# Turning the MLP's input block by block on the chip, and storing it turned, in an FNet layer with a channel MLP

## The chip, the cores and the metric

One core of a Trainium2 chip runs the whole layer as one program. The metric is the device time of one execution in microseconds (us). Profiled executions add a trace: every instruction's start and duration on TensorE (PE for matmuls, PEld for weight loads), VectorE (DVE), ScalarE (ACT), GpSimd (POOL) and SyncE (SP), and every DMA. SP computes nothing here: it is the queue that issues nearly all DMAs, in order. POOL issues most of the stores to memory. "SPq" and "POOLq" in a row mean a DMA being issued from that queue.

## The reference, cut to what matters

```python
def reference(...):
    # x: 2048 tokens x 1024; six modulation rows from silu(c) @ w_mod
    h = layernorm(x) * (1 + ca) + sa
    a, b = h @ dft_hid_re.T, h @ dft_hid_im.T
    x = x + ga * (dft_seq_re @ a - dft_seq_im @ b)
    h = layernorm(x) * (1 + cb) + sb
    z = layernorm(h)                       # the MLP's own norm
    g = gelu(z @ w1 + b1)                  # 1024 -> 3584
    return x + gb * (g @ w2 + b2)          # 3584 -> 1024
```

## The kernel before, in words

All matrix products are float32 products done in float16: each operand is split into a high and a low half ("hi" is written by ACT, "lo" by DVE), and each product is made in three passes (hi hi, hi lo, lo hi). On top of that every product of 2 x 2 quadrants is done with seven products instead of eight (m = 0 to 6, in the order `ORDER` = 0, 1, 2, 4, 3, 6, 5). A piece is 12 matmuls of 128x512.

The stages, in order of time:

- **First stages**, to about 657 us: the DFT over the sequence (lines 1109 and 1159).
- **GEMM2** (line 1377), 657 to 961 us: the DFT over the hidden axis, in eight blocks b = 0 to 7 of 256 tokens. A block is 14 pieces. Each piece reads a `u` operand that SP loads from memory into a ring of eight places (line 1329), so a load waits until the piece eight before it is done. ACT copies (line 1393) and DVE adds (line 1399) bring the result from PSUM to `y`.
- Behind each block run the two layer norms, "LN b" (`ln_tasks`: DVE lines 1250 to 1273, ACT lines 1209, 1221, 1276), and then `z_tasks(b)`: seven operands of z, each 128 tokens x (hi, lo) x 512 values in float16, 256 KB. Their hi is ACT line 383, their lo DVE line 393, the combinations between them DVE line 408. POOL stores each to memory in `zc_d` (line 1310). LN b needs the residual rows of x, which SP loads (`load_xw`, line 1351) once the place is free that z b-2 was made from.
- **GEMM3 and GEMM4**, from 961 us (lines 1543 and 1652): the MLP. Tokens 0 to 1023 (blocks 0 to 3, h = 0) go through all 14 chunks of the hidden axis, gemm3(0) to gemm3(13), and then tokens 1024 to 2047 (h = 1), gemm3(14) to gemm3(27). The contraction runs over the values of a token, so z must have its values on the partitions: it must be turned. `load_zc(h, m)` (line 1319) does that with one DMA transpose of 1 MB from memory for each m. Those of h = 0 are issued in the last block of GEMM2, into places that the hidden-DFT operand `dp` held; those of h = 1 during gemm3(13), as each m of it is done.
- gemm3(0) and gemm3(1) run beside LN 6, LN 7 and z 6 and 7. In a gemm3, ACT copies (line 1565) and DVE adds (line 1569) empty the PSUM banks; three m go into bank "a" one after the other, so the copy after m = 0 must be done before m = 2 begins, and the add after m = 3 before m = 5.

What sets the order of the instructions on each engine is a planner in the kernel's Python: tasks with a price, dependences and a due time wait in streams, and `fill_to` emits the one that could start first by the planner's own clocks. The chip then runs each engine's list strictly in order. `need` forces all tasks of a tag out, `emitted` those of a key. `store(ring, n, ...)` pushes a store that must be emitted before slot n of a ring of buffers is used again.

Of the kernel before, what the change touches and what calls it, by code (L numbers as in the profile page):

```python
# [9 lines left out]
F16 = mybir.dt.float16  # L10
# [6 lines left out]
P = 128  # L17
S = 2048
D = 1024
# [15 lines left out]
def kernel(ctx, tc, x, cre, cim, dre, dim, w1, b1, w2, b2, c, wm, out):  # L35
# [137 lines left out]
    def quad(g):  # L173
# [45 lines left out]
    streams = {}  # L219
# [981 lines left out]
    def ln_tasks(b):  # L1201

        y, w, cl = yb(b), wb(b), lns[b % 2]
        su, nm, v, ve, r, a = (cl[:, n, :] for n in range(6))
        junk = at(180, 1024, F16)

        def norm(src, scale):
            def square(n):
# [82 lines left out]
    def z_tasks(b):  # L1291

        e, o = zw(b)[:, 0], zw(b)[:, 1]
        q = [e[:, 0:512], o[:, 0:512], e[:, 512:1024], o[:, 512:1024]]
        places = [O_K + 8 + 2 * k for k in range(4)] if b == NB - 1 else [144, 146, 148, 150, 152, 154]
        h, k = divmod(b, 4)
        n, at_ = [0], {}

        def outs(m):
            at_[m] = n[0]  # L1300
            reuse("z", (b, n[0] - len(places)) if n[0] >= len(places) else None)
            if n[0] < len(places) and 0 < b < NB - 1:
                need(f"z{b - 1}")
            v = at(places[n[0] % len(places)], 1024, F16).rearrange("p (a x) -> p a x", a=2)
            n[0] += 1
            return v[:, 0], v[:, 1], v
# [5 lines left out]
        return right_tasks(  # L1312
            q, outs, None, 512, lambda j: ("w", b, j % 2), lambda m: ("z", b, m), post=post,
            free=lambda m: slot("z", lambda: (b, n[0] - len(places))),
        )

    def load_zc(h, m):
        o = at(O_ZC[m], 4096, F16).rearrange("p (n t) -> p n t", t=P)
        sp.dma_start_transpose(o, zc_d[h][m].rearrange("p a k c e -> p (a k c e)"))

    def load_up(N):
        b, n = divmod(N, NP)
# [208 lines left out]

    for b in range(NB):
        gemm2(b, each(b))
        push("ln", "ln", ln_tasks(b), clk["pe"] + 10.0)
# [5 lines left out]
    def product3(ps, s, m, start):  # L1540
        for d in range(4):
            for n, (a, b) in enumerate(PASSES):
                pe.matmul(  # L1543
                    ps.rearrange("p (k t) -> p k t", k=4),
                    w1c[:, m, s, a, d * P : (d + 1) * P],
                    zc(m)[:, b, :, d, :],
                    start=(start and d == 0 and n == 0),
                    stop=(d == 3 and n == 2),
                    skip_group_check=not start,
                )  # L1550
# [271 lines left out]
    for kind, k in seq:  # L1822
        if kind == 3:
# [4 lines left out]
            if g == 0:  # L1828
# [1 line left out]
                    f = lambda m=m: sp.dma_start(w1c[:, m, 0], w1_d[2][:, m])  # L1830
                    Task("dma", 0.75, f, key=("w1", 2, m)).run()
                load_w1(3, *range(4))
                push("z", f"z{NB - 2}", z_tasks(NB - 2), due[3, 1] + 5)
                push("hid", "hid0", hid_tasks(0), due[3, 1] + 0)
            elif g == 1:
                need(f"z{NB - 2}", "ln", "st_w2", "st_x2")
# [91 lines left out]
```

## Time and profile before

| | |
|---|---|
| Median of 3 runs | 2008.03 us (2007.22 to 2009.2) |
| The profiled execution | 2008.09 us, its span 2006.3 us |
| PE busy | 1964.1 us (98%), 8954 matmuls |
| DVE busy | 1418.4 us (71%) |
| ACT busy | 835.0 us (42%) |
| POOL busy | 189.7 us (9%) |
| DMA | 402.39 MB in 195136 packets, mean 201 GB/s |

Busy shares are averages over stages with different limits; PE's row says that 42 us of the span have no matmul in them, and the granted clock (a column of the stage table) says where a matmul took longer than its usual 0.216 us. A timeline row has start, duration, engine, line, operation, tiles and count, and in brackets how long the engine sat idle before it and what ended that. A row of a stage table has the stage, its length, busy time and count of PE, PEld, DVE, ACT and POOL, the granted clock, the busy share of the 16 DMA engines and GB/s.

### The profile page before, as it was taken

The numbers are of one execution on the slowest core, as the hardware profiler recorded it, in microseconds if no ns is written. First come the engines' busy times: TensorE is split into PE (matmuls) and PEld (weight loads), VectorE is DVE, ScalarE is ACT, GpSimd is POOL, SyncE is SP. The second block draws the span as 40 slices with busy tenths as digits, with TensorE's granted clock in tenths as the row PEclk, the third lists the DMA queues.
The fourth block names the chain that finished last, engine by engine and source line by source line (L and its number), as shares of the span: only waits on it lengthen the run. The fifth ranks groups of instructions, "written<-read, shape, count | busy, mean of one in ns | idle before, by whom it ended". The sixth has DMA issues, their size and how long they took to land.

```text
span 2006.3 us, 23428 instructions
## 1 busy us (share of the span) xinstructions
PE 1964.1 (98%) x8954; PEld 883.5 (44%) x8954; DVE 1418.4 (71%) x1795; ACT 835.0 (42%) x1075; POOL 189.7 (9%) x280
## 2 busy tenths in 40 slices
PE   9999999999999999998889999999999999999998
PEld 3444444444444444443334444444444444444443
DVE  2977886997884478776488899999864354553566
ACT  2853432344542254543367566466323322212311
POOL 0002202221210022121020000000000000000000
PEclk9999999999999999999889999999999999999999
DMA  9138677788678877879856454444497333432323
GB/s 383 47 110 281 218 268 273 264 303 325 244 273 331 306 246 267 285 263 270 211 191 204 160 201 169 145 169 153 112 255 225 119 92 93 121 102 72 110 74 84
DMA packets 195136, 402.39 MB, mean 201 GB/s; under 512 B 73104, under 2 KB 73104, under 8 KB 192208
## 3 DMA queue, kind: packets, MB, share of 16 engines
q1 hardware_dynamic: 168304, 309.92, 47.0%
q0 software_dynamic: 26720, 90.98, 12.8%
q8 instruction: 70, 1.15, 0.2%
q14 instruction: 42, 0.34, 0.1%
HBM read 248.27 MB, written 137.89 MB: 192 GB/s over the span
## 4 chain that ended last, share of the span: by engine, by line
PE 84%; DVE 9%; DMA 3%; issue 2%; ACT 1%; SPq 0%; POOL 0%; DVEq 0%; POOLq 0%; ACTq 0%
PE ps L1543 23%; PE ps L1652 23%; PE ps L1159 18%; PE ps L1377 13%; PE ps L1109 5%; DVE arena L681 1%; PE ps L471 1%; DVE arena L630 1%; DVE arena L631 1%; DVE arena L395 1%; DMA arena<-zc 1%; DVE arena L1698 1%; DVE arena L633 1%; DMA arena<-in_wm_dram 1%; PE ps L477 1%
## 5 line engine op out<-in xcount | busy, mean ns | idle before, releaser
L1543 PE MATMUL ps<-arena 128*128 128x512 f16 x2352 | 515.9, 382 | 17.7 <-ACT arena L1565 8.9
L1652 PE MATMUL ps<-arena 128*128 128x512 f16 x2352 | 510.8, 379 | 1.3 <-DVE sums L908 0.5
L1159 PE MATMUL ps<-arena 128*128 128x512 f16 x2016 | 435.5, 379 | 0.8 <-DMA arena<-s 0.8
L1543 PEld LDWEIGHTS <-arena 128*128 128x128 f16 x2352 | 231.0, 98 | 300.5 <-issue 16.5
L1652 PEld LDWEIGHTS <-arena 128*128 128x128 f16 x2352 | 229.9, 98 | 279.9 <-issue 1.7
L1698 DVE SCALAR_TENSOR_TENSOR arena<-ps,i4c,arena 128x1024 f32<-128x1024 f32 x179 | 229.4, 1282 | 148.2 <-PE ps L1652 146.2
L1377 PE MATMUL ps<-arena 128*128 128x512 f16 x1344 | 294.4, 382 | 9.1 <-DMA arena<-u 8.3
L1159 PEld LDWEIGHTS <-arena 128*128 128x128 f16 x2016 | 197.1, 98 | 239.0 <-DMA arena<-s 1.7
L383 ACT ACTIVATE arena<-arena,shc 128x512 f16<-128x512 f32 (+1 forms) x115 | 115.9, 1018 | 276.5 <-PE ps L1652 184.6
L1377 PEld LDWEIGHTS <-arena 128*128 128x128 f16 x1344 | 132.2, 98 | 171.1 <-DMA arena<-u 9.3
L1109 PE MATMUL ps<-arena 128*128 128x512 f16 x768 | 167.4, 379 | 7.3 <-ACT arena L632 2.0
L408 DVE TENSOR_TENSOR arena<-arena 128x512 f32<-128x512 f32 (+1 forms) x228 | 171.1, 754 | 4.4
L678 ACT ACTIVATE arena<-arena 128x1024 f16<-128x1024 f32 x100 | 104.1, 1050 | 152.1 <-PE ps L1159 113.3
L395 DVE SCALAR_TENSOR_TENSOR arena<-arena,shc 128x512 f16<-128x512 f32 (+1 forms) x115 | 128.7, 1122 | 34.8 <-ACT arena L383 34.6
L681 DVE SCALAR_TENSOR_TENSOR arena<-arena 128x1024 f16<-128x1024 f32 x100 | 128.7, 1305 | 18.9 <-ACT arena L678 18.9
L1569 DVE TENSOR_TENSOR arena<-arena,ps 128x512 f32<-128x512 f32 x84 | 57.5, 686 | 110.9 <-PE ps L1543 105.9
L1562 ACT ACTIVATE arena<-arena,b1s,i1c 128x512 f32<-128x512 f32 x84 | 68.3, 813 | 149.5 <-DVE arena L1569 149.5
L1109 PEld LDWEIGHTS <-arena 128*128 128x128 f16 x768 | 74.7, 98 | 100.0 <-ACT arena L632 4.0
L770 ACT ACTIVATE arena<-arena 128x1024 f16<-128x1024 f32 x56 | 57.7, 1047 | 59.3 <-DVE arena L1183 19.3
L773 DVE TENSOR_TENSOR arena<-arena 128x1024 f16<-128x1024 f32 x56 | 66.9, 1219 | 14.7 <-ACT arena L770 14.7
L383 ACT ACTIVATE arena<-arena,s1c 128x512 f16<-128x512 f32 (+1 forms) x70 | 60.7, 884 | 37.0 <-DVE arena L408 24.2
L1565 ACT ACTIVATE arena<-ps 128x512 f32<-128x512 f32 x84 | 49.7, 592 | 59.2 <-PE ps L1543 58.0
(153 smaller groups left out, 1387.2 us busy)
## 6 DMA issues: line engine op xcount, KB each, us to landing
w<-arena SPq DMA_DIRECT2D x64, 512.0 KB, 4.9
arena<-w SPq DMA_DIRECT2D x119, 256.0 KB, 2.7
u<-arena POOLq DMA_DIRECT2D x56, 512.0 KB, 5.3
arena<-u SPq DMA_DIRECT2D x112, 256.0 KB, 4.1
arena<-w SPq DMA_DIRECT2D x56, 512.0 KB, 3.4
arena<-s SPq DMA_DIRECT2D x48, 512.0 KB, 7.6
arena<-in_cre_dram SPq DMA_DIRECT2D x32, 512.0 KB, 7.1
arena<-in_cim_dram SPq DMA_DIRECT2D x32, 512.0 KB, 5.9
```

The lines of the kernel that those rows point to most:

```text
L383: act.activation(o[m][0], q(j), AF.Copy, **sc)
L395: dve.scalar_tensor_tensor(o[m][1], q(j), scale, o[m][0], op0=ALU.mult, op1=ALU.subtract)
L408: dve.tensor_tensor(q(d), q(a), q(b), op=op)
L678: h = Task("act", 1.15, lambda: act.activation(o[:, :, 0], s2, AF.Copy, scale=SC), list(deps) + free)
L681: dve.scalar_tensor_tensor(o[:, :, 1], s2, SC, o[:, :, 0], op0=ALU.mult, op1=ALU.subtract)
L1109: pe.matmul(bank_of(d_), hleft(d_, s, kp, a), cop(n)[:, s, b], start=(kp == 0 and s == 0 and a == 0 and b == 0), stop=(kp == 7 and s == 1 ...
L1159: pe.matmul(bank_of(st + ch), left, cop(n)[:, s, b], start=(start and kp == 0 and s == 0 and a == 0 and b == 0), stop=(kp == 3 and s == 1 ...
L1377: pe.matmul(bank_of(bk), up(N)[:, c_, a], dp(n)[:, c_, w], start=(start and ri == 0 and c_ == 0 and i == 0), stop=(ri == 1 and c_ == 3 and ...
L1543: pe.matmul(ps.rearrange("p (k t) -> p k t", k=4), w1c[:, m, s, a, d * P : (d + 1) * P], zc(m)[:, b, :, d, :], start=(start and d == 0 and ...
L1562: act.activation(dst, src, AF.Gelu_apprx_tanh, scale=inv, bias=b1s[:, 2 * p + j : 2 * p + j + 1])
L1652: pe.matmul(t[:, j], hidc[:, c_, m, a, k * P : (k + 1) * P], w2c[:, m, c_, w], start=(start and c_ == 0 and n == 0), stop=(c_ == 1 and n = ...
L1698: lambda: dve.scalar_tensor_tensor(dst, ps[b], inv, dst, op0=ALU.mult, op1=ALU.add), kp[b],
```

## The change

Each z operand of blocks 0 to 6 is turned as soon as its lo half is written: SP issues a DMA transpose of the 256 KB from SBUF to SBUF (128x8x128), and POOL stores the turned copy. The MLP's load for h = 0 is then a plain 1 MB copy; that of h = 1 is a plain 768 KB copy and one 256 KB transposing load, for block 7 alone, which is stored unturned in its own tensors `zl_d`. Buffers: the untransposed operand has four places (six before), free again when its transpose has landed; the turned one has five (four for block 6), free again when POOL's store has landed. So the hi of operand 4, 5 or 6 of a block waits for the transpose of operand 0, 1 or 2, and the transpose of operand 5 for the store of operand 0. The tasks of block 6 are no longer pushed behind gemm3(0) but with the others, behind GEMM2's block; LN 7's scratch row moves to another address; `need` goes round again when a forced task pushes another.

```diff
     def zc(m):
-        return at(O_ZC[m], 4096, F16).rearrange("p (a k c t) -> p a k c t", a=2, k=4, c=4)
+        return at(O_ZC[m], 4096, F16).rearrange("p (k a c t) -> p k a c t", k=4, a=2, c=4)
...
     zc_d = [
-        [dram.tile([P, 2, 4, 4, P], F16, tag=f"zc_{h}_{m}", name=f"zc_{h}_{m}") for m in range(7)] for h in range(2)
+        [dram.tile([P, 4 - h, D], F16, tag=f"zc_{h}_{m}", name=f"zc_{h}_{m}") for m in range(7)] for h in range(2)
     ]
+    zl_d = [dram.tile([P, D], F16, tag=f"zl_{m}", name=f"zl_{m}") for m in range(7)]
...
     def need(*tags):
 
-        for q in list(streams.values()):
-            while any(t.tag in tags for t in q):
-                force(q, q[0])
+        while any(t.tag in tags for q in streams.values() for t in q):
+            for q in list(streams.values()):
+                while any(t.tag in tags for t in q):
+                    force(q, q[0])
...
-        places = [O_K + 8 + 2 * k for k in range(4)] if b == NB - 1 else [144, 146, 148, 150, 152, 154]
+        end = b == NB - 1
+        places = [(O_K + 8 if end else 144) + 2 * k for k in range(4)]
+        turned = [152, 154, 216, 218] + [182] * (b < NB - 2)
...
+        def gone(i):
+            return ("st", "z", (b, i)) if end else ("tz", b, i)
...
         def post(m, o_):
-            dst = zc_d[h][m][:, :, k].rearrange("p a c e -> p a (c e)")
-            store("z", (b, at_[m]), lambda: gp.dma_start(dst, o_[2]), ("z", b, m), f"z{b}")
+            i, v = at_[m], o_[2]
+            if end:
+                store("z", (b, i), lambda: gp.dma_start(zl_d[m], v), ("z", b, m), f"z{b}")
+                return
+            o = at(turned[i % len(turned)], 1024, F16)
+
+            def turn():
+                if i >= len(turned):
+                    emitted(("st", "z", (b, i - len(turned))))
+                sp.dma_start_transpose(o.rearrange("p (n t) -> p n t", t=P), v)
+                store("z", (b, i), lambda: gp.dma_start(zc_d[h][m][:, k], o), gone(i), f"z{b}")
+
+            LANDS[gone(i)] = 2.5
+            free = [("st", "z", (b, i - len(turned)))] if i >= len(turned) else []
+            push("tz", f"z{b}", [Task("dma", 1.3, turn, [("z", b, m), *free], gone(i))], clk["dve"])
...
     def load_zc(h, m):
-        o = at(O_ZC[m], 4096, F16).rearrange("p (n t) -> p n t", t=P)
-        sp.dma_start_transpose(o, zc_d[h][m].rearrange("p a k c e -> p (a k c e)"))
+        o, d = at(O_ZC[m], 4096, F16), zc_d[h][m].rearrange("p k x -> p (k x)")
+        if h == 0:
+            sp.dma_start(o, d)
+        else:
+            sp.dma_start(o[:, 0 : 3 * D], d)
+            sp.dma_start_transpose(o[:, 3 * D :].rearrange("p (n t) -> p n t", t=P), zl_d[m])
...
-        if b < NB - 2:
+        if b < NB - 1:
             push("z", f"z{b}", z_tasks(b), clk["pe"] + 40.0)
...
-                push("z", f"z{NB - 2}", z_tasks(NB - 2), due[3, 1] + 5)
+                need(f"ln{NB - 2}", f"z{NB - 3}")
```

In the rows below, line numbers of the changed kernel are higher than those of the kernel before for the same line (1329 becomes 1355, 1319 becomes 1327 for the turn and 1342 for the load, 1351 becomes 1377, 1565 becomes 1591, 1569 becomes 1595, 1209 becomes 1211, 1276 becomes 1278, 383 becomes 385).

First place: SP's queue in the last block of GEMM2, around its last three `u` loads (`u_6_1`, `u_5_0`, `u_5_1`); `w_0` and `w_1` are chunks 0 and 1 of w1. Before:

```order
L1329 DMA arena_65<-u_6_0_139 128x1024
L1319 DMA_TRANSPOSE arena_65<-zc_0_67 128x32x128
L1527 DMA arena_65<-w_1_161 128x1024
L1329 DMA arena_65<-u_6_1_140 128x1024
L1319 DMA_TRANSPOSE arena_65<-zc_1_68 128x32x128
L1527 DMA arena_65<-w_1_161 128x1024
L1329 DMA arena_65<-u_5_0_137 128x1024
L1319 DMA_TRANSPOSE arena_65<-zc_2_69 128x32x128
L1527 DMA arena_65<-w_1_161 128x1024
L1329 DMA arena_65<-u_5_1_138 128x1024
```

The same place in the changed kernel; its transposes are those of block 5's operands:

```order
L1355 DMA arena_65<-u_6_0_146 128x1024
L1342 DMA arena_65<-zc_0_67 128x4096
L1553 DMA arena_65<-w_1_168 128x1024
L1355 DMA arena_65<-u_6_1_147 128x1024
L1342 DMA arena_65<-zc_1_68 128x4096
L1553 DMA arena_65<-w_1_168 128x1024
L1327 DMA_TRANSPOSE arena_65<-arena_65 128x8x128
L1355 DMA arena_65<-u_5_0_144 128x1024
L1327 DMA_TRANSPOSE arena_65<-arena_65 128x8x128
L1342 DMA arena_65<-zc_2_69 128x4096
L1553 DMA arena_65<-w_1_168 128x1024
L1355 DMA arena_65<-u_5_1_145 128x1024
```

Three transposes of 1 MB ahead of the last `u` load have become three copies of 1 MB and two transposes of 256 KB.

Second place: SP's queue a little further on, around the load of x for LN 7. Before:

```order
L1319 DMA_TRANSPOSE arena_65<-zc_4_71 128x32x128
L1527 DMA arena_65<-w_1_161 128x1024
L1319 DMA_TRANSPOSE arena_65<-zc_3_70 128x32x128
L1527 DMA arena_65<-w_1_161 128x1024
L1319 DMA_TRANSPOSE arena_65<-zc_6_73 128x32x128
L1527 DMA arena_65<-w_1_161 128x1024
L1351 DMA arena_65<-in_x_dram 128x2x1024
L1319 DMA_TRANSPOSE arena_65<-zc_5_72 128x32x128
```

And after:

```order
L1327 DMA_TRANSPOSE arena_65<-arena_65 128x8x128
L1342 DMA arena_65<-zc_4_71 128x4096
L1553 DMA arena_65<-w_1_168 128x1024
L1327 DMA_TRANSPOSE arena_65<-arena_65 128x8x128
L1342 DMA arena_65<-zc_3_70 128x4096
L1553 DMA arena_65<-w_1_168 128x1024
L1327 DMA_TRANSPOSE arena_65<-arena_65 128x8x128
L1342 DMA arena_65<-zc_6_73 128x4096
L1553 DMA arena_65<-w_1_168 128x1024
L1327 DMA_TRANSPOSE arena_65<-arena_65 128x8x128
L1377 DMA arena_65<-in_x_dram 128x2x1024
L1342 DMA arena_65<-zc_5_72 128x4096
```

Between the last `u` load and the load of x stood three transposes of 1 MB; now four of 256 KB and three copies of 1 MB stand there.

Third place: ACT's queue from the last gelu of gemm3(1) to the first copy of gemm3(2) (the bottom row), beside LN 7. Before:

```order
L1562 ACTIVATE arena_65<-ps,b1s_203,i1c_207 128x512
L383 ACTIVATE arena_65<-arena_65,shc_208 128x2x512
L383 ACTIVATE arena_65<-arena_65 128x512 x2
L1276 ACTIVATE arena_65<-arena_65,lns_34_213 128x1024 x2
L383 ACTIVATE arena_65<-arena_65 128x512 x3
L892 ACTIVATE ps,sums_6644<-arena_65 128x1024 x2
L383 ACTIVATE arena_65<-arena_65,shc_208 128x512
L383 ACTIVATE arena_65<-arena_65,shc_208 128x2x512
L1565 ACTIVATE arena_65<-ps 128x512
```

And after, where `shc` marks the hidden operand of GEMM4 and 128x1024 with `lns` the steps of LN 7:

```order
L1588 ACTIVATE arena_65<-ps,b1s_210,i1c_214 128x512
L1211 ACTIVATE arena_65,lns_34_220<-arena_65,lns_34_220 128x1024 x2
L385 ACTIVATE arena_65<-arena_65,shc_215 128x2x512
L1278 ACTIVATE arena_65<-arena_65,lns_34_220 128x1024 x2
L894 ACTIVATE ps,sums_6700<-arena_65 128x1024
L385 ACTIVATE arena_65<-arena_65,shc_215 128x512
L385 ACTIVATE arena_65<-arena_65,shc_215 128x2x512
L1591 ACTIVATE arena_65<-ps 128x512
```

Five hi halves of block 6 have left the stretch ahead of the copy, and two squares of LN 7, which stood ahead of the last gelu, have come into it.

More of the change, by code (lines that the diff above doesn't have):

```diff
@@ L1204, in ln_tasks @@
         su, nm, v, ve, r, a = (cl[:, n, :] for n in range(6))
-        junk = at(180, 1024, F16)
+        junk = at(O_K + 8 if b == NB - 1 else 180, 1024, F16)
         def norm(src, scale):
@@ L1294, in z_tasks @@
         q = [e[:, 0:512], o[:, 0:512], e[:, 512:1024], o[:, 512:1024]]
-        places = [O_K + 8 + 2 * k for k in range(4)] if b == NB - 1 else [144, 146, 148, 150, 152, 154]
+        end = b == NB - 1
+        places = [(O_K + 8 if end else 144) + 2 * k for k in range(4)]
+        turned = [152, 154, 216, 218] + [182] * (b < NB - 2)
         h, k = divmod(b, 4)
         n, at_ = [0], {}
+        def gone(i):
+            return ("st", "z", (b, i)) if end else ("tz", b, i)
         def outs(m):
-            at_[m] = n[0]
-            reuse("z", (b, n[0] - len(places)) if n[0] >= len(places) else None)
-            if n[0] < len(places) and 0 < b < NB - 1:
+            i = at_[m] = n[0]
+            if i >= len(places):
+                emitted(gone(i - len(places)))
+            elif 0 < b < NB - 1:
@@ L1303, in outs @@
                 need(f"z{b - 1}")
-            v = at(places[n[0] % len(places)], 1024, F16).rearrange("p (a x) -> p a x", a=2)
+            v = at(places[i % len(places)], 1024, F16)
             n[0] += 1
-            return v[:, 0], v[:, 1], v
+            w = v.rearrange("p (a x) -> p a x", a=2)
+            return w[:, 0], w[:, 1], v
         def post(m, o_):
-            dst = zc_d[h][m][:, :, k].rearrange("p a c e -> p a (c e)")
-            store("z", (b, at_[m]), lambda: gp.dma_start(dst, o_[2]), ("z", b, m), f"z{b}")
+            i, v = at_[m], o_[2]
@@ L1312, in z_tasks @@
+            free = [("st", "z", (b, i - len(turned)))] if i >= len(turned) else []
+            push("tz", f"z{b}", [Task("dma", 1.3, turn, [("z", b, m), *free], gone(i))], clk["dve"])
         return right_tasks(
             q, outs, None, 512, lambda j: ("w", b, j % 2), lambda m: ("z", b, m), post=post,
-            free=lambda m: slot("z", lambda: (b, n[0] - len(places))),
+            free=lambda m: lambda: gone(n[0] - len(places)) if n[0] >= len(places) else None,
         )
     def load_zc(h, m):
-        o = at(O_ZC[m], 4096, F16).rearrange("p (n t) -> p n t", t=P)
@@ L1545, in product3 @@
                     w1c[:, m, s, a, d * P : (d + 1) * P],
-                    zc(m)[:, b, :, d, :],
+                    zc(m)[:, :, b, d, :],
                     start=(start and d == 0 and n == 0),
```

4 lines of the change are left out of this document (2 added, 2 removed).

## The prediction

> **What bounds the kernel now.** I read the page's chain first, then PE's waits, then PE's timeline at the places the waits name.
>
> ```profile
> span 2006.3 us, 23428 instructions
> PE 84%; DVE 9%; DMA 3%; issue 2%; ACT 1%; SPq 0%; POOL 0%; DVEq 0%; POOLq 0%; ACTq 0%
> ```
>
> PE is the bound nearly everywhere, so only time in which PE stands still or runs slowly can be won. PE's timeline around the end of GEMM2 and at the second load of z:
>
> ```profile
> 899.69 43.55 PE L1377 MATMUL ps<-arena 128*128 128x512 f16 x201
> 947.17 4.19 PE L1377 MATMUL ps<-arena 128*128 128x512 f16 x12 [3.93 <-DMA arena<-u]
> 955.74 5.01 PE L1377 MATMUL ps<-arena 128*128 128x512 f16 x12 [4.39 <-DMA arena<-u]
> 981.12 27.57 PE L1543 MATMUL ps<-arena 128*128 128x512 f16 x120 [4.83 <-DVE arena L1569]
> 1017.63 15.14 PE L1543 MATMUL ps<-arena 128*128 128x512 f16 x60 [8.94 <-ACT arena L1565]
> ```
> ```profile
> 1464.19 7.10 PE L1543 MATMUL ps<-arena 128*128 128x512 f16 x24 [3.03 <-DMA arena<-zc]
> 1472.20 2.76 PE L1543 MATMUL ps<-arena 128*128 128x512 f16 x12 [0.91 <-DMA arena<-zc]
> ```
>
> The first row gives the undisturbed matmul: 43.55 / 201 = 0.2167 us, a piece of 12 = 2.60. Behind each wait the matmuls are slower than that, so a wait costs twice. Four losses, wait plus excess:
> - the last two `u` pieces: 3.93 + 1.59 + 4.39 + 2.41 = 12.3 us;
> - an add of gemm3(0): 4.83 + (27.57 - 26.00) = 6.4;
> - the first copy of gemm3(2): 8.94 + (15.14 - 13.00) = 11.1;
> - the reload for the second half: 3.03 + 1.90 + 0.91 + 0.16 = 6.0.
>
> Together 35.8 us, all that the change can win here.
>
> **What stands behind each.** SP's timeline in the first:
>
> ```profile
> 921.45 0.42 SPq L1329 DMA_DIRECT2D arena<-u  x1
> 925.13 5.68 SPq L1319 DMA_TRANSPOSE arena<-zc  x1
> 930.86 0.57 SPq L1527 DMA_DIRECT2D arena<-w  x1
> 931.48 0.45 SPq L1329 DMA_DIRECT2D arena<-u  x1
> 932.10 8.05 SPq L1319 DMA_TRANSPOSE arena<-zc  x1
> ```
>
> and, of the rows that follow, the last two loads of `u` and that of x:
>
> ```profile
> 940.82 0.43 SPq L1329 DMA_DIRECT2D arena<-u  x1
> 949.28 0.92 SPq L1329 DMA_DIRECT2D arena<-u  x1
> 970.57 0.39 SPq L1351 DMA_DIRECT2D arena<-in_x_dram  x1
> ```
>
> A transpose of 1 MB holds SP for 5 to 8 us, while a copy (L1527) holds it 0.57. The last three `u` loads stand behind one each; the last two come 949.28 - 921.45 = 28 us after `u_6_0`, where PE eats three pieces in 7.8. The x load of LN 7 stands behind six of them, and DVE and PE wait for it:
>
> ```profile
> 976.63 1.23 DVE L1250 SCALAR_TENSOR_TENSOR arena<-arena 128x1024 f32<-128x1024 f32 x1 [8.84 <-DMA arena<-in_x_dram]
> ```
>
> The add after m = 3 (L1569), on which PE waits until 981.12, stands behind LN 7's add of x in DVE's list. So the first two losses are SP's time for transposes, and so is the fourth: its seven hold SP 19.09 + 14.92 us for what PE uses up in 7 x 2.60.
>
> ```profile
> 1435.29 19.09 SPq L1319 DMA_TRANSPOSE arena<-zc  x4
> 1455.11 14.92 SPq L1319 DMA_TRANSPOSE arena<-zc  x3
> ```
>
> The third is something else: ACT's copy at 1017 stands in its list behind LN 7's and GEMM4's steps. Of DVE's rows those on the way to it, from the last add of gemm3(1) on:
>
> ```profile
> 1000.96 0.69 DVE L1569 TENSOR_TENSOR arena<-arena,ps 128x512 f32<-128x512 f32 x1
> 1003.66 0.17 DVE L1215 TENSOR_SCALAR lns<-lns 128x2 f32<-128x2 f32 x1
> 1006.39 2.35 DVE L1261 TENSOR_TENSOR arena<-arena 128x1024 f32<-128x1024 f32 x2
> 1009.98 1.42 DVE L408 TENSOR_TENSOR arena<-arena 128x512 f32<-128x512 f32 x2
> 1013.18 1.28 DVE L395 SCALAR_TENSOR_TENSOR arena<-arena,shc 128x1024 f16<-128x1024 f32 x1
> ```
>
> and LN 7's shift, before that add, with ACT's last rows on the way:
>
> ```profile
> 992.83 1.28 DVE L1256 SCALAR_TENSOR_TENSOR arena<-arena,lns 128x1024 f32<-128x1024 f32 x1
> 1002.40 1.14 ACT L1209 ACTIVATE arena<-arena,lns 128x1024 f16<-128x1024 f32 x1
> 1015.22 1.87 ACT L383 ACTIVATE arena<-arena,shc 128x512 f16<-128x512 f32 x2 [0.63 <-DVE arena L408]
> 1017.00 0.58 ACT L1565 ACTIVATE arena<-ps 128x512 f32<-128x512 f32 x1
> ```
>
> **The change, part by part.** *The price of a 256 KB transpose.* No row has one from SBUF; the nearest are the 14 of 1 MB from memory, and the 256 KB copies for the landing:
>
> ```profile
> L1319 SPq DMA_TRANSPOSE arena<-zc x14: 4250/5376/8047, 925.1 to 1465.6; - x14
> DMA to landing us min/median/max: 6.4/8.5/13.9
> arena<-u SPq DMA_DIRECT2D x112, 256.0 KB, 4.1
> ```
>
> On SP a quarter of the data is a quarter of the time if it scales: 1.06 to 2.01, median 1.34 us. If it doesn't scale, 5.38. I take 1.34, since a copy of 1 MB (the load of x, 0.39) and one of 256 KB (`u`, 0.42 to 0.92) cost SP alike and the transposes far more, so theirs goes by the data; the ends are kept. From issue to landing I take 4 us, the copies' 4.1; the other end is the 1 MB median, 8.5.
>
> *SP in GEMM2.* A block of 14 pieces is 14 x 2.60 = 36.4 us. SP holds 14 `u` loads x 0.45 = 6.3 us, an x load and up to four weight loads some 2; seven transposes add 7 x 1.34 = 9.4. That is 18 of 36, and a `u` load is issued eight pieces = 20.8 us ahead of its use, so one or two transposes in front of it (2.7 us) and its landing (4.1) are covered by 14 us. Cost nothing. A transpose also waits for DVE's lo, and the `u` loads behind it on SP wait with it; the cover is the same 14 us.
>
> *ACT and POOL.* The hi of operand 4 now waits for the transpose of operand 0 to land, and behind it in ACT's list stand the PSUM copies. In block 1 of z:
>
> ```profile
> 772.49 1.29 DVE L393 TENSOR_TENSOR arena<-arena 128x512 f16<-128x512 f32 x2 [3.69 <-ACT arena L383]
> 782.20 1.14 ACT L383 ACTIVATE arena<-arena 128x512 f16<-128x512 f32 x2
> ```
>
> The first lo ended about 773.1 and the pair of hi with the first reuse began at 782.2, 9 us later, against 1.3 + 4 for turn and landing. Later operands follow closer, so I expect waits of a microsecond or two there; a PSUM copy behind them has a piece, 2.6 us, to spare. POOL's stores wait for the transposes too, with nobody near behind them.
>
> *The DMA engines.* Busy share and GB/s of stages: copies alone, GEMM2, and mostly transposes:
>
> ```profile
> 600.00:650.00 50.00, 50.00 (x233) 22.69 (x232) 24.85 (x22) 12.38 (x13) 2.17 (x5) 1.00 0.84 340
> 750.00:800.00 50.00, 50.00 (x233) 22.69 (x232) 38.71 (x76) 23.03 (x39) 10.25 (x18) 1.00 0.80 274
> 800.00:850.00 50.00, 49.17 (x229) 22.20 (x227) 37.22 (x70) 27.73 (x43) 10.15 (x17) 1.00 0.82 289
> 1445.00:1450.00 5.00, 5.00 (x25) 2.27 (x24) 4.09 (x5) 1.63 (x2) 0.00 (x0) 1.00 0.99 188
> 1450.00:1455.00 5.00, 5.00 (x25) 2.29 (x24) 4.74 (x6) 4.16 (x5) 0.00 (x0) 1.00 1.09 242
> ```
>
> Copies move 340 / 0.84 = 405 GB/s at full share, transposes 188 / 0.99 = 190 to 242 / 1.09 = 222. A 0.262 MB transpose thus holds all engines 1.18 to 1.38 us, seven of them 9 us of a 36.4 us block: +0.25 on shares of 0.80 and 0.82, so 1.05 and 1.07. Over the two stages of GEMM2 shown the excess over 1 is at most 0.05 x 50 + 0.07 x 50 = 6 us, the least is none; a gain is excluded but for the 0.83 us that PE lacks in 800 to 850. I take 2 us lost, near the low end, since `u`'s cover absorbs single delays.
>
> [...]
>
> *The last `u` loads.* Copies of 1 MB, at 0.57 us on SP as above, replace transposes. Counting from 925.1: the last `u` load is issued after three such copies, three weight copies, two `u` loads and two small transposes, 3 x 0.57 + 3 x 0.57 + 2 x 0.45 + 2 x 1.34 = 7.0, about 932. `dp`'s places may come free late; the first transpose here at 925.13 shows that the first was free by then, and I allow 2 us more. Issued at 934 and landing with the 1 MB transposes' 6.4 to 8.5, it is there by 942.5, and PE, 943.2 at the piece before it (947.17 - 3.93), needs it at 943.2 + 2.6 = 945.8. All 12.3 us are won.
>
> *The load of x.* Four more small transposes, three copies of 1 MB and weights stand before it: they hold SP 4 x 1.34 + 6 x 0.57 = 8.8 us behind 934, and I estimate 946 with waits for places, some 25 us earlier than at 970.57. The load issued at 970.57 let DVE go on at 976.63, 6 us later; with 6 to 11 it is there at 952 to 957, or later where the engines are full. PE now ends GEMM2 at 948.4, and the add after m = 3 must be done at 948.4 + 6 x 2.60 = 964.0; between x and that add DVE has 5.7 us (two 1.2 us rows of LN, two lo, two combinations, the add). So x may come at 958. I take 1 us lost, 5.4 won; bounds 6.4 and 0.
>
> *The copy of gemm3(2).* Here the changed order has LN 7's shift (L1256) behind the last add of gemm3(1), and z 6 out of the way. From that add: 0.69 + 2 x 1.28 + two squares 2.6 + root 2.73 (1003.66 to 1006.39) + 2.35 + lo 1.28 + combinations 1.42 + two hi 1.87 + copy 0.58 = 16.1 us, where before it took 1017.58 - 1000.96 = 16.6. PE needed the copy 16.6 - 8.94 = 7.7 behind the add. So it waits 8.4 again, in place of 8.94, and slows behind it again: 0.5 won, not 11.1. What is taken off DVE here (z 6) has been replaced by LN 7, which earlier stood ahead.
>
> *The reload.* SP needs 0.57 + 1.34 an operand, the engines 0.786 / 405 + 1.3 = 3.3 us; seven are in by 1435.3 + 23 + 4 = 1462, the last is needed at 1450.6 + 6 x 2.60 = 1466. All 6.0 won.
>
> Sum: 12.3 + 5.4 + 0.5 + 6.0 - 2 = 22.2, so 2008.1 - 22.2 = 1985.9 us, against the profiled execution's 2008.09, which stands 0.06 above the median of the runs.
>
> **The rivals.**
> - *The copy's wait goes too* (LN 7 gets ahead because x comes 25 us earlier, while DVE sat idle 8.84 us for it): 8.4 + 2.1 more, 1975.4 us. Against it: the adds of gemm3(1) stand in DVE's list ahead of the shift, so LN 7 cannot run ahead of PE.
> - *The engines are full*: 6 us lost in GEMM2 and x late enough to keep the whole 6.4: 1985.9 + 4 + 5.4 + 2 for `u` = 1997.3. For it: shares of 1.07.
> - *Slower: the transpose from SBUF doesn't scale.* SP then is the bound. The point: 36.4 - 8.3 = 28 us a block for seven, 4.0 us each. At 5.38, a block takes 8.3 + 37.7 = 46 us, 9.6 more; six blocks issue transposes, less 20.8 of cover: +37, and nothing won: 2045. [...]
> - *No change*: transposes near 3 to 4 us, delays eating the 22.
>
> **Chances.** Forecast 0.62 (1980 to 1992); copy's wait gone 0.11; engines full 0.14 (1992 to 2002); no change 0.04; slower 0.09. 0.2%, 4 us, is about what a measurement here can tell. Faster 0.87, same 0.04, slower 0.09. The range 1974 to 2000 holds the forecast, nearly all of the second and most of the third.
>
> **What would show it.** Small transposes of 1.1 to 2 us on SP; no PE wait on `u` at the end of GEMM2; x issued before 955; the wait on ACT's copy in gemm3(2) still there, 7 to 9 us; no wait on `zc` in gemm3(14); shares near 1 in GEMM2. Small transposes beyond 4 us on SP, or landings beyond 10, would make it wrong.

## The result: slower by about 1%, and the profile after

| | median, us | ratio to the kernel before in the same chip run, 95% interval |
|---|---|---|
| the kernel before | 2007.7 (2007.22 to 2009.2) | 1 |
| the changed kernel | 2030.3 (2024.6 to 2034.2) | 1.0109 (1.0084 to 1.0134) |
| the same, again on another chip run | 2023.0 (2019.9 to 2028.0) | 1.0075 (1.0055 to 1.0096) |

The forecast was 1985.9 us, faster. The first lines of the changed kernel's page are its span and the shares of the chain of work that ended last:

```profile
span 2027.9 us, 23528 instructions
PE 74%; DMA 11%; DVE 10%; issue 2%; ACT 2%; SPq 0%; POOL 0%; POOLq 0%; DVEq 0%; ACTq 0%
```

DMA's share of the chain has grown from 3% to 11% in this execution. (In the second trace of the same kernel the chain could be followed over little more than half of the span, so this share is a hint and no more.) PE's timeline from the middle of GEMM2 to the first GEMM4, with the idle time before each row and what ended it in brackets:

```profile
824.15 38.10 PE L1403 MATMUL ps<-arena 128*128 128x512 f16 x168 [6.77 <-ACT arena L1419]
868.58 38.07 PE L1403 MATMUL ps<-arena 128*128 128x512 f16 x168 [6.33 <-ACT arena L1419]
908.63 38.11 PE L1403 MATMUL ps<-arena 128*128 128x512 f16 x168 [1.98 <-ACT arena L1419]
949.23 17.39 PE L1403 MATMUL ps<-arena 128*128 128x512 f16 x72 [2.49 <-ACT arena L1419]
968.45 5.34 PE L1403 MATMUL ps<-arena 128*128 128x512 f16 x24 [1.84 <-ACT arena L1419]
978.95 8.11 PE L1403 MATMUL ps<-arena 128*128 128x512 f16 x24 [5.16 <-DVE arena L1425]
986.90 41.60 PE L1569 MATMUL ps<-arena 128*128 128x512 f16 x192
1036.18 14.59 PE L1569 MATMUL ps<-arena 128*128 128x512 f16 x60 [7.68 <-ACT arena L1591]
1079.82 2.75 PE L1678 MATMUL ps<-arena 128*128 128x512 f16 x12 [0.56 <-ACT arena L1714]
1087.22 6.90 PE L1678 MATMUL ps<-arena 128*128 128x512 f16 x24 [4.66 <-ACT arena L1714]
```

No wait on `u` is left, and none on the add behind LN 7's x: 192 matmuls of gemm3(0) and gemm3(1) run in one piece. The copy of gemm3(2) still makes PE wait, 7.68 us. Later, the second load of z costs nothing any more; gemm3(13) and gemm3(14), 84 matmuls each, run without a gap:

```profile
1459.81 36.42 PE L1569 MATMUL ps<-arena 128*128 128x512 f16 x168
```

What is new are six waits on ACT and DVE in GEMM2, where before the two on `u` stood at its end, and one in gemm4(0). In GEMM2 PE now waits 24.6 us in place of 9.1, and its matmuls take 300.5 us in place of 294.3, since they run slower behind the longer waits (168 take 38.10 us behind the first, where the same number without one takes 36.42; granted clock 0.96 over the stage, 0.98 before). By stages, in us (ends taken from the first matmul of the next stage; gemm3(13) and gemm3(14) from the first's first matmul to the next stage's; each trace is of one execution):

| stage | before | after | after, again | change in the first profile |
|---|---|---|---|---|
| up to GEMM2 | 657.2 | 661.8 | 658.3 | +4.6 |
| GEMM2 | 303.4 | 325.1 | 319.2 | +21.7 |
| gemm3(0) to the first GEMM4 | 72.0 | 63.7 | 65.1 | -8.3 |
| gemm4(0) | 36.3 | 43.3 | 43.8 | +7.1 |
| gemm3(13) and gemm3(14) | 42.3 | 36.3 | 36.3 | -6.0 |
| the rest, 2.1 of it waits in the GEMM4 at 1203 | | | | +2.7 |

The sum is the 21.8 us between the two profiled times (2029.9 and 2008.1). The first line belongs to that execution: up to GEMM2 every engine's list is that of the kernel before, and all sixteen other profiles of this study begin GEMM2 between 656.3 and 658.9.

**How a transpose comes to stop PE.** One of the waits, from four engines' timelines, in the order in which it happened: DVE's adds that make the rows of x ready for their store, SP's transpose of z's last operand, POOL's three issues, ACT's copy.

```profile
848.69 2.35 DVE L1263 TENSOR_TENSOR arena<-arena 128x1024 f32<-128x1024 f32 x2
850.30 2.67 SPq L1327 DMA_TRANSPOSE arena<-arena  x1
853.46 0.56 POOL L1264 DMA_DIRECT2D out_dram<-arena  x1
861.30 0.55 POOL L1328 DMA_DIRECT2D zc<-arena  x1 [7.28 <-DMA arena<-arena]
861.92 0.55 POOL L1264 DMA_DIRECT2D out_dram<-arena  x1
867.93 0.60 ACT L1419 ACTIVATE arena<-ps 128x512 f32<-128x512 f32 x1 [8.70 <-DMA out_dram<-arena]
```

The second row of x was ready at 851.0. Its store stands in POOL's list behind the store of the turned operand, and that waits for the transpose, issued at 850.30 and landed at about 861.2. So the store of x goes out at 861.92, eleven us after its data was there. ACT's copy writes into the rows that this store still reads, so it waits until the store has landed, and PE goes on at 868.58. The second way is shorter: ACT's own hi halves wait for a place, that is, for the transpose of the operand four before, with the copies behind them in ACT's list:

```profile
965.82 0.63 ACT L385 ACTIVATE arena<-arena 128x512 f16<-128x512 f32 x1 [6.52 <-DMA arena<-arena]
975.68 0.63 ACT L385 ACTIVATE arena<-arena 128x512 f16<-128x512 f32 x1 [7.28 <-DMA arena<-arena]
```

These two are behind the waits at 968 and 979 us, the first through ACT's copy, the second through DVE's lo half, behind which the add stands in DVE's list. The transposes' own row, what waited for them, and their landing:

```profile
L1327 SPq DMA_TRANSPOSE arena<-arena x49: 1242/1574/6700, 738.0 to 1019.8; - x49
  POOL zc L1328: 191.2, 40
  ACT arena L385: 22.0, 9
DMA to landing us min/median/max: 3.1/5.9/10.8
```

By the median they cost on SP about what was forecast (1.57 us against 1.34). But the 42 in GEMM2 add up to 95.2 us there, 2.27 each, and they land after 6.3 us by the median (5.9 for all 49), up to 10.8.

### The profile page after: what moved, and what is told of

The parts are those of the page before. It is cut to its first block, busy times and chain, and to the rows that moved or that the text cites. A ratio compares the mean times of both kernels' runs of the same rounds, so it can differ in the third digit from the quotient of the medians.

```text
span 2027.9 us, 23528 instructions
## 1 busy us (share of the span) xinstructions
PE 1970.1 (97%) x8954; PEld 885.4 (44%) x8954; DVE 1418.6 (70%) x1795; ACT 838.6 (41%) x1075; POOL 179.1 (9%) x280
## 4 chain that ended last, share of the span: by engine, by line
PE 74%; DMA 11%; DVE 10%; issue 2%; ACT 2%; SPq 0%; POOL 0%; POOLq 0%; DVEq 0%; ACTq 0%
PE ps L1678 23%; PE ps L1569 23%; PE ps L1161 15%; PE ps L1403 6%; PE ps L1111 5%; DMA arena<-arena 4%; DMA arena<-in_wm_dram 2%; DMA out_dram<-arena 2%; PE ps L473 1%; DMA w<-arena 1%; DVE arena L397 1%; DVE arena L683 1%; DVE arena L410 1%; DVE arena L632 1%; DVE arena L633 1%
## 5 line engine op out<-in xcount | busy, mean ns | idle before, releaser
L1403 PE MATMUL ps<-arena 128*128 128x512 f16 x1344 | 300.7, 387 | 24.6 <-ACT arena L1419 19.4
L397 DVE SCALAR_TENSOR_TENSOR arena<-arena,s1c 128x512 f16<-128x512 f32 (+1 forms) x70 | 66.4, 959 | 12.8 <-ACT arena L385 12.5
```

The lines of the kernel that those rows point to most:

```text
L397: dve.scalar_tensor_tensor(o[m][1], q(j), scale, o[m][0], op0=ALU.mult, op1=ALU.subtract)
L1403: pe.matmul(bank_of(bk), up(N)[:, c_, a], dp(n)[:, c_, w], start=(start and ri == 0 and c_ == 0 and i == 0), stop=(ri == 1 and c_ == 3 and ...
```

## The experiments

Two theories at first: Q, the queues (POOL's list, with stores behind stores that wait for a transpose), and E, the DMA engines being full. A GEMM2 time below is that of one profiled execution; the other times are medians. "Stores on SP" below is always the same move: the stores of x and of the w1 and w2 operands.

**1. POOL no longer waits for transposes.**

```diff
-store("z", (b, i), lambda: gp.dma_start(zc_d[h][m][:, k], o), gone(i), f"z{b}")
+store("z", (b, i), lambda: gp.dma_start(zc_d[h][m][:, k], v), gone(i), f"z{b}")
```

> The changed kernel with one argument changed: the stores of z on POOL take the unturned operand, so they wait for DVE's lo and no longer for the transpose to land. The turned copy is made all the same and thrown away (the values stored are not turned), so the DMA engines carry the same bytes and every engine's list is the same. Theory Q (POOL's queue: the stores of x and w1 stand behind stores of z that wait for a transpose, and ACT's PSUM copies behind those): the four waits of GEMM2 that end on ACT's copy, 24.6 us with what PE loses behind them, go, the two on ACT's hi waiting for a place (10.1 us) stay: about 2006 us. Theory E (the DMA engines are full, at shares of 0.94 to 1.10, and everything lands late): nothing changes, about 2030.

Measured: 2011.2 us, ratio 1.0009 (0.9997 to 1.0021); GEMM2 312.7 us (its execution, 2016.3 us, is the slowest of ten). The first way loses its POOL part; the waits on ACT's copy are smaller, but do not go:

```profile
PE ps L1403 <- ACT arena L1419: 13.2, 5, 3.7
```

In the changed kernel this line reads 19.4 us in 5 waits, 6.8 the longest. Theory Q explains most, not all: transposes landed still later here (median 7.2 us).

**2. Plain copies for transposes.**

```diff
-sp.dma_start_transpose(o.rearrange("p (n t) -> p n t", t=P), v)
+sp.dma_start(o, v)
```

> The changed kernel with the 49 transposes from SBUF to SBUF replaced by plain copies of the same 256 KB between the same places (z is not turned). Same lists otherwise. Theory Q: what matters is how long a turn takes to land; a copy lands in some 4 us in place of 5.9, so the waits shrink by a third to a half: 2010 to 2018 us. Theory E: the share of the DMA engines falls by 0.1 to 0.2 in GEMM2 and nearly all of its loss goes: about 1990. A third theory, P (the new order of the planner on ACT and DVE is at fault, whatever the transposes do): 2030.

Measured: 1999.4 us, ratio 0.9955 (0.9940 to 0.9970); GEMM2 297.7 us. The lists, the bytes and the order are the same, so the new order alone is not the cause (theory P falls), and the turning itself costs some 24 to 31 us. The time lies between the numbers of Q and E. A stage table's row for GEMM2, of the changed kernel and of this one (the last two columns are the busy share of the DMA engines and GB/s):

```profile
661.82:986.90 325.08, 300.51 (x1346) 133.77 (x1345) 206.23 (x370) 132.23 (x205) 47.18 (x86) 0.96 0.95 289
657.38:955.11 297.73, 290.88 (x1346) 131.49 (x1345) 203.98 (x362) 130.62 (x204) 47.88 (x85) 1.00 0.88 314
```

The engines were busy for 0.95 x 325.1 = 308.8 us with 42 transposes in that stage, and for 0.88 x 297.7 = 262.0 with 42 copies: by these shares a transpose holds all engines some 46.8 / 42 = 1.1 us longer than a copy of the same 256 KB. A rival is not parted from this: a copy also holds SP for 0.47 us only, and the copies land after 5.0 us, not much before the transposes' 5.9. So part of the lateness may lie ahead of the issue, on SP, and no run separates SP's time from the engines'.

**3. The stores on SP.**

```diff
-store("x2", 2 * b + n, lambda: gp.dma_start(out[2 * b + n], y[:, n]), ...)
+store("x2", 2 * b + n, lambda: sp.dma_start(out[2 * b + n], y[:, n]), ...)
-(gp if g < 3 else sp).dma_start(w1_d[g][:, span(m)], o[2])
+sp.dma_start(w1_d[g][:, span(m)], o[2])
...
```

> The changed kernel with the stores of x and of the w1 and w2 operands that POOL issued among those of z (two of 512 KB and some four a block) issued by SP at the same point of the program; POOL keeps the stores of z. ACT's, DVE's and PE's lists are the same. Theory Q: the copies no longer wait for stores behind those of z: the 24.6 us go, some come back where SP waits for DVE ahead of u loads: 2006 to 2012 us. Theory E: about 2030, since the same bytes move.

Measured: 2009.3 us, ratio 0.9998 (0.9987 to 1.0010); GEMM2 308.2. Theory Q's number: with the same transposes and the same bytes the program is, by the ratios, 15 to 22 us faster than the changed kernel's two measurements. Of the 19.4 us of waits on ACT's copy in GEMM2 8.8 are left:

```profile
PE ps L1403 <- ACT arena L1419: 8.8, 3, 4.3
```

But the program only comes level with the kernel before: what it was to win is still lost.

**4. A planner that expects late landings.**

```diff
-LANDS[gone(i)] = 2.5
+LANDS[gone(i)] = 8.0
```

> The changed kernel with one number of the planner changed: a turned operand counts as landed 8.0 us behind its issue, not 2.5 (the traces show 3.1 to 10.8, median 5.9). That lets the planner put stores of z and the hi halves that reuse a place later in the lists. Theory Q: most of the 24.6 us and part of the 10.1 go: 2000 to 2012 us. Theories E and P: within 5 us of 2030.

Measured: 2026.5 us, ratio 1.0086 (1.0071 to 1.0101). Missed by all numbers of theory Q; by the number alone, theories E and P have it right. GEMM2 did get shorter, 312.4 us, but the delayed steps ran into gemm3(0) and gemm3(1), which took 79.7 us where the changed kernel took 63.7:

```profile
989.18 4.61 PE L1569 MATMUL ps<-arena 128*128 128x512 f16 x12 [6.09 <-ACT arena L1591]
997.77 28.74 PE L1569 MATMUL ps<-arena 128*128 128x512 f16 x120 [3.98 <-DVE arena L1595]
```

**5. Neither list is meant to wait, the engines carry the same.**

```diff
-places = [(O_K + 8 if end else 144) + 2 * k for k in range(4)]
-turned = [152, 154, 216, 218] + [182] * (b < NB - 2)
+places = [(O_K + 8 if end else 144) + 2 * k for k in range(4 if end else 6)]
+turned = [216, 218] + [182] * (b < NB - 2)
-if i >= len(turned): emitted(("st", "z", (b, i - len(turned))))
...
```

The stores take `v`, as in 1.

> As the run with unturned stores (stores of z take the unturned operand, the turned copy is thrown away), and besides the unturned operand has six places as before the change, and the transposes write into two or three places of their own and wait for no store. So neither POOL nor, nearly, ACT's hi halves wait for a transpose; the DMA engines carry what they carry in the changed kernel. Theory QH (the loss is made by two lists that wait for a landing: POOL's stores and ACT's hi halves): with both gone GEMM2 takes 292 to 296 us and the program 1990 to 1996. Theory E (full DMA engines cost by themselves, through u and x): GEMM2 stays above 302, the program above 2002.

Measured: 2021.4 us, ratio 1.0069 (1.0048 to 1.0090); GEMM2 305.9. Theory QH missed; both of theory E's bounds are met. But this is no clean cell: the order moved with the places, and ACT's hi halves still wait 20.4 us for transposes, nearly all of it in two:

```profile
953.61 0.63 ACT L385 ACTIVATE arena<-arena 128x512 f16<-128x512 f32 x1 [8.19 <-DMA arena<-arena]
985.68 1.15 ACT L385 ACTIVATE arena<-arena 128x512 f16<-128x512 f32 x2 [11.28 <-DMA arena<-arena]
```

One place speaks for the engines by themselves. POOL's issue of a row of x, ACT's copy and PE's restart:

```profile
846.24 0.53 POOL L1264 DMA_DIRECT2D out_dram<-arena  x1 [1.74 <-DVE lns L1217]
858.77 0.60 ACT L1418 ACTIVATE arena<-ps 128x512 f32<-128x512 f32 x1 [4.56 <-DMA out_dram<-arena]
859.42 5.93 PE L1402 MATMUL ps<-arena 128*128 128x512 f16 x16 [10.22 <-DMA arena<-u]
```

Nothing that waits stood ahead of this store, and it took some 12 us to land, in a stretch where the engines' share was about 1 (0.98 from 840 to 860 us, 1.10 from 800 to 850). That the share is the reason is a reading, not shown apart. (PE's wait is put down to `u`; the copy ended at 859.37, just before PE went on.) In the kernel before, these stores landed after 4.2 us, 6.0 at most; in the changed kernel after 6.6, 9.8 at most:

```profile
L1262 POOL DMA_DIRECT2D out_dram<-arena x16: 534/540/557, 721.8 to 1009.2; - x16
DMA to landing us min/median/max: 2.9/4.2/6.0
L1264 POOL DMA_DIRECT2D out_dram<-arena x16: 534/540/563, 726.5 to 1032.5; - x16
DMA to landing us min/median/max: 3.5/6.6/9.8
```

**6 and 7. One half alone.** Blocks 0 to 3 only, and blocks 4 to 6 only:

```diff
+keep4 = end or b > 3
-return ("st", "z", (b, i)) if end else ("tz", b, i)
+return ("st", "z", (b, i)) if keep4 else ("tz", b, i)
-if end: store("z", (b, i), lambda: gp.dma_start(zl_d[m], v), ...)
+if keep4: store("z", (b, i), lambda: gp.dma_start(zc_d[1][m][:, k], v), ...)
...
```

The loads of the half that is stored unturned are transposes of 1 MB again, and its unturned operands have six places. The diff is that of run 6; run 7 sets `keep4 = end or b < 4`.

> Only blocks 0 to 3 (h = 0) are turned on the chip; blocks 4 to 6 are stored unturned from six places, and the loads of h = 1 are transposes of 1 MB from memory, as before the change. If the losses of GEMM2 belong to the blocks that are turned: against the changed kernel without its chance delay (2025) the waits at 909 to 979 us go (17.7 us with what follows them) and the wait at the reload comes back (6.0): 2013 us. If the loss comes from the new order of the lists or from the engines being full at the end of GEMM2, whichever block is turned: 2025 to 2031.

> The other half alone: only blocks 4 to 6 (h = 1) are turned on the chip; blocks 0 to 3 are stored unturned from six places, and the loads of h = 0 are transposes of 1 MB in the last block of GEMM2, as before the change. By the sum over places: 2008 + 17.7 (waits at 909 to 979 us) + 7.1 (the new wait in gemm4(0)) - 6.0 (reload) = 2027, less what the two kinds of waits at the end of GEMM2 share; 2015 to 2027. If all seven blocks are needed for the engines to be full: 2002 to 2008.

Measured: 2021.1 us, ratio 1.0062 (1.0041 to 1.0084), and 2017.0 us, ratio 1.0046 (1.0031 to 1.0061). Each half costs by itself, though half of the blocks are left alone; the first lies between its two numbers, the second in its range. Blocks 0 to 3 lengthen GEMM2 (314.4 us), blocks 4 to 6 spoil its end (309.0).

**8. Blocks 0 to 3 with the stores on SP** (6 and 3 together).

> Blocks 0 to 3 alone turned on the chip, and the stores of x and of the w1 and w2 operands issued by SP in place of POOL, so that nothing stands behind a store of z. By theory QH: the run with blocks 0 to 3 alone, less most of its two waits on ACT's copy in GEMM2 (16 us): 1997 to 2003, faster than the kernel before. If SP's waits for DVE delay the u loads as much: 2010.

Measured: 2004.4 us, ratio 0.9981 (0.9972 to 0.9991); GEMM2 300.4. A little better than the kernel before, and 17 us below run 6: the size that the queue theory has for the move, though the time lies 1.4 us above its range.

**9 and 10. The fourth cell and the control.** Copies with the stores on SP (2 and 3 together), and the kernel before with the stores on SP.

> The changed kernel with plain copies for its 49 transposes (z is not turned) and with the stores of x and of the w1 and w2 operands on SP: the fourth cell of a table whose others are 2030 (transposes, stores on POOL), 2009 (transposes, stores on SP) and 1999 (copies, stores on POOL). If the two causes multiply (a late landing hurts because stores stand behind it in POOL's list): the stores' move is worth a few us once landings are short: 1992 to 1998. If they add: 2030 - 21 - 31 = 1978. If each removes the same loss by itself and another remains: 1999.

> The kernel before with the stores of x and of the w1 and w2 operands on SP: the control for that move. In the kernel before POOL's stores of z wait only for DVE, so both theories expect no gain: 2006 to 2012 us.

Measured: 1992.9 us, ratio 0.9927 (0.9911 to 0.9944), and 2009.3 us, ratio 1.0001 (0.9990 to 1.0013). As ratios to the kernel before:

| | stores on POOL | stores on SP |
|---|---|---|
| transposes | 1.0075 and 1.0109 | 0.9998 |
| copies | 0.9955 | 0.9927 |
| neither (before) | 1 | 1.0001 |

Moving the stores is worth 0.8 to 1.1% where transposes stand in POOL's way, 0.3% where copies do, nothing in the kernel before. So the two causes do not add; they multiply: with the transposes landings are later (their own 5.9 us, where the copies' are 5.0; the stores of x 6.6, where they are 5.9 in run 2), and the lists hand the lateness on to PE. With copies and the stores on SP GEMM2 takes 293.7 us, where 1344 matmuls at the undisturbed 0.2167 us are 291.2, and of the waits on ACT's copy this is left:

```profile
PE ps L1403 <- ACT arena L1419: 2.0, 1, 2.0
```

Against run 9, run 3 still loses 0.7%, or 14 us, to the transposes.

**11, 12 and 15. Turning only what is worth it.** From the kernel before: of blocks 0 to 3, only the operands that the MLP loads first, m = 0, 1, 2 (and 4 in the last run), each with a place of its own (operand 4 takes operand 0's, once that is stored); stores on SP in the last two.

```diff
+if h == 1 or m not in (0, 1, 2):
     store("z", (b, at_[m]), lambda: gp.dma_start(dst, o_[2]), ("z", b, m), f"z{b}")
+    return
+o = at((216, 218, 182)[(0, 1, 2).index(m)], 1024, F16)
+    sp.dma_start_transpose(o.rearrange("p (n t) -> p n t", t=P), v)
+    store("z", (b, i), lambda: gp.dma_start(dst, src), ("tz", b, i), f"z{b}")
+LANDS["tz", b, i] = 6.0
...
```

The transpose is a task of its own, and the MLP's loads of these operands are plain copies.

> The kernel before with only three of the seven operands (m = 0, 1, 2, the first three that the MLP loads) of only blocks 0 to 3 turned on the chip: 12 transposes of 256 KB in place of 49, each with a place of its own, the planner told that they land 6 us behind their issue. Three loads of 1 MB ahead of the last u loads become copies, and the x load of LN 7 stands behind three transposes of 1 MB and not six. If the engines' time and the queues are what costs, the loss in GEMM2 shrinks to at most 12/46 of the changed kernel's 32 us, some 8, and the gain of 12.3 + 6.4 us at its end stays: 1990 to 2000 us. If any turning in GEMM2 costs its full waits: 2010 or more.

> The same with the stores of x and of the w1 and w2 operands on SP. Theory QH: no store stands behind a store of z, 0 to 6 us better than the run with three operands: 1988 to 1996 us. If the order of the lists has by itself dealt with the queue: the same as that run.

> The run with three operands of blocks 0 to 3 turned and the stores on SP (2001), with a fourth operand (m = 4) turned as well, so that the x load of LN 7 stands behind two transposes of 1 MB and not three. Its waits at 964 and 972 us (zc 2.4, and the add behind LN 7's add of x 6.0 and 1.5 behind it) shrink to 0 to 4 us if they are SP's time for the fourth transpose: 1994 to 1999. If the four more transposes of 256 KB cost as much in GEMM2: 2001.

Measured: 2004.4 us, ratio 0.9984 (0.9974 to 0.9993); 2001.2 us, 0.9966 (0.9954 to 0.9978); 1996.2 us, 0.9944 (0.9927 to 0.9961). The first two miss their ranges by 4 to 5 us, the third is in its own. GEMM2 takes 291.8, 291.4 and 292.5 us: 12 or 16 transposes cost next to nothing there, and the 11 us of `u` are won. What the first two lack is behind it, in gemm3(0), where the other four operands still come through transposes of 1 MB: from GEMM2's end to the first GEMM4 they take 77.8 and 75.8 us, where the kernel before took 72.0. With four operands turned it is 71.1. PE's last row of GEMM2 in run 12, without a wait on `u`, then PE's rows of the last run, and its small transposes:

```profile
849.78 98.58 PE L1395 MATMUL ps<-arena 128*128 128x512 f16 x456 [0.85 <-ACT arena L1411]
949.64 15.70 PE L1563 MATMUL ps<-arena 128*128 128x512 f16 x72
969.26 27.58 PE L1563 MATMUL ps<-arena 128*128 128x512 f16 x120 [3.91 <-DVE arena L1589]
1005.77 15.14 PE L1563 MATMUL ps<-arena 128*128 128x512 f16 x60 [8.93 <-ACT arena L1585]
L1322 SPq DMA_TRANSPOSE arena<-arena x16: 1237/1257/3280, 733.4 to 864.7; - x16
DMA to landing us min/median/max: 3.1/4.4/7.5
```

They land after 4.4 us, near the forecast's 4, though the engines' share was 0.97 and 1.02 from 750 to 850 us, where half of them run. So a full share does not tell by itself how late landings get, and how many of the 49 are too many stays open. This version beats both kernels, by 12 us the one before.

**13 and 14. Two open parts.** The changed kernel again, and the changed kernel with block 6's tasks pushed behind gemm3(0), as before the change (`if b < NB - 2` in place of `NB - 1`, and the push again at g = 0).

> The changed kernel unchanged, on another chip run. Its profile had 4.6 us of waits and slow matmuls at 316 and 437 us, in the DFT over the sequence, where its lists are those of the kernel before. If that was a chance of that execution, GEMM2 begins at 656 to 659 us here as in the twelve other profiles, and the profiled time follows GEMM2's waits alone; if it belongs to the change, at 661 or later.

> The changed kernel with the tasks of block 6 of z pushed behind gemm3(0), as before the change, in place of with the others. If the new loss of 7 us in gemm4(0) (ACT's copy from PSUM behind a norm step of w2 that waits for its load) comes from where the planner puts block 6 and what follows it: that wait goes, 2020 to 2024 us. If it comes from somewhere else in the change, the wait stays and the time is 2030 with at most 4 us either way.

Measured: 2023.0 us, GEMM2 from 658.3 on, so the 4.6 us were that execution's; and 2022.4 us, ratio 1.0062 (1.0038 to 1.0086), which the unaltered kernel's 1.0075 (1.0055 to 1.0096) does not part from. The number lies in the range for a wait that goes, and says nothing, since the unaltered kernel lies there too. In run 14 gemm4(0) took 41.0 us in place of 43.8, with the waits moved to others. In the first trace of the changed kernel ACT's copy in gemm4(0) stands behind a step of w2's norm (L894) that began at 1085.02 us, after ACT had stood idle for 5.25. What in the change makes this wait stays open. It is neither the transposes nor POOL's list, since run 9 has it too (43.4 us); the runs built on the old order, 10 to 12 and 15, do not have it (36.3).

## Why the prediction was wrong, step by step

- **"POOL's stores wait for the transposes too, with nobody near behind them"**: this step failed, and made the program slower in place of even. Behind them in POOL's list stood the stores of x and of the w1 operands, and ACT's copies from PSUM waited for those. The list had to be read through to who waits for each entry. Runs 3 and 10 show it: the same transposes cost 15 to 22 us less with those stores elsewhere, and in the kernel before the move is worth nothing. It is nearly half of the error of 37 to 44 us; the rest follows.
- **"From issue to landing I take 4 us"**: mis-sized. It was 5.9, up to 10.8; 4.4 in run 15, which makes 16. The other end, 8.5, was written down and not used for ACT or POOL.
- **"The excess over 1 is at most 6 us ... 2 us lost"**: the shares came out near the forecast's 1.05 and 1.07, but the step from share to time was wrong.

```profile
750.00:800.00 50.00, 50.00 (x234) 22.65 (x232) 35.40 (x75) 25.07 (x42) 9.72 (x18) 1.00 1.10 294
800.00:850.00 50.00, 43.23 (x193) 19.15 (x192) 34.67 (x62) 22.95 (x37) 8.16 (x15) 0.93 0.99 290
```

  At 1.10 PE lost nothing and at 0.99 nearly 7 us, so the loss is not the excess. Landings got later instead, stores of x from 4.2 to 6.6 us and `u` from 4.1 to 5.8, and each list that waits in order for one pays. Each transpose also held the engines longer than the forecast's 1.18 to 1.38 us: a copy's 0.262 MB at the 405 GB/s of before, 0.65 us, and run 2's 1.1 more make some 1.76, an estimate. By it a transpose moves its bytes at 0.65 / 1.76 = 0.37 of a copy's rate, well under half.
- **hi waiting "a microsecond or two"**: mis-sized. The last two waits, up to 7.3 us on ACT, cost PE about 10.
- **The last `u` loads, 12.3 won**: the wait went, as reasoned. In run 12 GEMM2 shows the win by itself, 303.4 to 291.4 us. In the changed kernel the new waits buried it.
- **x, 5.4 won**: the wait went, but in the changed kernel with some luck. x was to be issued before 955 us and was issued at 984.90, behind transposes that held SP for up to 5.7 us; PE was as late, so it cost nothing. In run 9, with copies, x comes at 946.04, as forecast, with GEMM2's end at 950.17 and no wait of PE:

```profile
984.90 0.52 SPq L1377 DMA_DIRECT2D arena<-in_x_dram  x1
946.04 0.38 SPq L1377 DMA_DIRECT2D arena<-in_x_dram  x1
```

- **The copy of gemm3(2), 0.5 won**: right; its wait stayed, at 7.68 us against the 8.4 forecast. With x, the stretch became 8.3 us shorter in place of 5.9.
- **The reload, 6.0 won**: right to the tenth, 42.3 to 36.3 us.
- **SP, 1.34 us a transpose**: right by the median, 1.57, and too low in the sum: 95.2 us for the 42 in GEMM2, where 42 x 1.34 is 56.3, with the longest at 6.70. The forecast's own signs of being wrong, transposes beyond 4 us on SP and landings beyond 10, were both there. No piece waited for `u`, so the slower rival that was priced, SP as the bound, was not what happened. No rival had POOL's list in it, and the "engines full" one stopped at 1997.
- **gemm4(0), +7.1**: not in the prediction at all.

So GEMM2, forecast 10.3 us shorter, was 16 to 22 longer. These 26 to 32 us are most of the error of 37 to 44; gemm4(0) is 7 more, and in the first measurement the 4.6 us of its own execution.

## What to carry to other kernels

A step that is moved onto a queue that issues in order must be followed through that queue: list what stands behind each of its waits, and who waits for that, two links on, above all stores whose landing frees a buffer. A busy share near 1 of the DMA engines was no rounding of the sum here: at 0.94 to 1.10, landings of `u` grew from 4.1 to 5.8 us and those of the stores of x from 4.2 to 6.6, and the engines that waited for them in order passed it on. If a transfer is moved to relieve one place, move only what that place needs: here 16 of the 49 transposes, with the stores on SP, gave 12 us where all 49 with the stores on SP gave nothing.

## What was not expected of the hardware

A transpose from SBUF to SBUF of 256 KB held the engines some 1.1 us longer than a copy between the same places (an estimate, from the shares 0.95 and 0.88 of GEMM2 in one execution of each), while SP's time for it was 1.57 us by the median, against 5.38 for one of 1 MB from memory, roughly as the data. And times spread: eight executions of the changed kernel lay between 2019.9 and 2034.2 us, the four of each kernel with copies within 2.3 us of each other (1998.7 to 2000.9 and 1992.4 to 1994.3). Why stays open; the kernel before, whose engines' share in GEMM2 is 0.82, also spread, from 2005.7 to 2015.3 us over 21 executions.
